# Attention and a two-layer feed-forward on one core: the last pair's first tile stored whole, and a new hand-written order of all operations

## The chip, the cores and the metric

The kernel runs on one core of one Trainium2 chip. The core has a matrix engine (TensorE, PE in the profile, with its weight loads shown apart as PEld), three engines for elementwise work (VectorE or DVE, ScalarE or ACT, GpSimd or POOL) and SyncE (SP), which only starts transfers. Each engine works through its own queue in order, and engines wait for each other by semaphores. Transfers (DMA) are started from the queues of SP, ACT and POOL. The metric is the device time of one execution in microseconds (us), lower is better.

## What is computed

Attention with a squared ReLU in place of a softmax, over 8 batches, 12 heads, 448 positions and head size 64; its output, as 3584 tokens of 768 features, goes through two weight matrices with a sigmoid-gated activation between them.

```
def _attn_ref(q, k, v):                       # each (8, 12, 448, 64)
    scores = scale * np.matmul(q, k.transpose(0, 1, 3, 2))
    attn = np.maximum(scores, 0.0) ** 2 / S
    return np.matmul(attn, v).astype(np.float32)

def _moe_ref(x, w_in, w_out):                 # (3584, 768), (768, 2048), (2048, 768)
    h = x @ w_in
    g = h * (1.0 / (1.0 + np.exp(-1.702 * h)))
    return (g @ w_out).astype(np.float32)
```

## The kernel before

**Units and batches.** Four heads of one batch make a unit u; there are 24 units, three to a batch. For each unit q and k are loaded, cast to fp16, transposed on TensorE (tq, tk) and copied out of PSUM (eq, ek). For each of seven row tiles j, TensorE makes the scores (s, four matmuls in 64x64 pieces of the array), ACT or DVE takes the ReLU of the two halves (r), ACT or DVE squares both at once (x), and after the seventh tile TensorE multiplies by v (a, 28 matmuls in 64x64 pieces). Two copies (e) bring the result into the batch's input for the feed-forward.

**First weight matrix.** For batch 0 it is a plain product: f (two matmuls of one third of the depth), then the activation g on ACT, then the widening v (scale and cast to fp16) on DVE or POOL into a ring buffer of two batches. For batches 1 to 7 it is a fast scheme with seven products in place of eight: sums of weight blocks (S, once) and of input blocks (T, per batch) on DVE, the products u (six matmuls each) on TensorE, a snapshot t of one bank on ACT or DVE, an addition b on DVE, then g and v.

**Second weight matrix.** The same scheme over pairs of 128-token tiles: sums W of weight blocks (once), sums A of the ring (per pair), the products p (eight matmuls each), snapshots h and final additions l into the output tile osb, and the stores o (a whole tile, on SP) or q (a part of a tile, on SP or ACT). A pair m covers the tiles m and m+1; the last pair is 26 with tiles 26 and 27. Its product p26.5 is split into two halves of 192 columns, p26.5.0 and p26.5.1, and l26.5 with it.

**The order.** `with tc.manual_schedule()` (from line 387 on) holds one long list of words, `words` (from line 430); `do` (line 404) issues them in exactly this order. Each engine's queue is the list's words for that engine, in the order of the list. A word is a name, its indices, an optional engine after a colon (`a` ACT, `d` DVE, `p` POOL) and, after an @, the PSUM banks that it takes into use. `r3.0.1` is the ReLU of unit 3, tile 0, half 1, on ACT (the default of r); `r3.0.0:d` is one on DVE; `s0.1@4.5` makes the scores of unit 0, tile 1 in banks 4 and 5. Without a suffix e, x, b, l, S, T, W and A are on DVE, r, t, h on ACT, g always on ACT, v on POOL. L loads q or k over SP, and K and Q cast what it loaded (default ACT for K, POOL for Q); j and V load with a cast over POOL's queue, jwa/jwb and jo the weights. A bank is taken again only after the operations that read it are through; buffers in SBUF (15 for at, 5 for gf, 3 for osb, 4 for v16 and so on) likewise.

The transposes come in two shapes: seven matmuls of 128x128 for units that were cast by K or Q, fourteen of 128x64 for units 1 to 5, which were loaded with a cast.

**The steps that the change touches at the end.** `store_part` (line 302) stores a part of a tile; its first index after the pair is h: 0 and 1 the halves of 384 columns, 2 and 3 quarters of 192. The index i picks the tile's upper or lower 64 rows, since these lie in different places of the output. With `:a` the store is started from ACT's queue, otherwise from SP's. `pair_snap` (line 362, word h) writes a scaled copy of a bank to osb, `pair_last` (line 366, word l) adds a bank to what osb holds; which of the two comes first on a piece of osb writes it, and the second one adds (`from_bank`, line 352). The end of the list, with the words of the last pair:

```
p26.4 l26.3 p26.6 h26.4:d h26.5 q27.1.1:a
q27.1.0 p26.5.0@4 q26.0.1:a l26.6 p26.5.1@3 q26.1.1:a q26.1.0 l26.5.0 q27.2.1:a
q27.2.0 l26.5.1 q27.3.1:a q27.3.0
```

Of the kernel before, what the change touches and what calls it, by code (L numbers as in the profile page):

```python
# [15 lines left out]
def kernel(  # L16
# [11 lines left out]
    NT, DM = out.shape  # L28
# [5 lines left out]
    NOUT = DM // 2  # L34
# [253 lines left out]
    lo, hi = slice(0, NOUT), slice(NOUT, DM)  # L288
# [13 lines left out]
    def store_part(e, p, m, h, i):  # L302
        b, j = divmod(2 * m + i, J)
        r0 = b * S + j
        c = slice(h * NOUT, (h + 1) * NOUT) if h < 2 else slice(
            (h - 2) * NOUT // 2, (h - 1) * NOUT // 2)
        (nc.scalar if e == "a" else nc.sync).dma_start(
            out=out[r0:r0 + 63 * J + 1:J, c], in_=osb[m][64 * i:64 * i + 64, c])
# [78 lines left out]
    with tc.manual_schedule():  # L387
# [34 lines left out]
        def zeros(e, p, n):  # L422
# [8 lines left out]
            "Lq0 Lk0 z9@0 jq1 jk1 I V0 V1 z1 Q0:d z1 z1 z1 z1 z1 z1 tq0@1 K0:d eq0:a tk0@2 ek0 "  # L431
            "tq1@3 jk2 eq1 s0.1@4.5 jq2 s0.4@6.7 s0.5@0.1 r0.1.1 r0.1.0:d s0.0@2.3 jq3 r0.5.1 "
            "r0.5.0:d s0.6@5.4 r0.0.0 r0.0.1:d r0.6.0 s0.2@1.0 x0.5 r0.2.0 s0.3@2.3 tk1@5 r0.2.1 "
            "x0.1 r0.4.0 ek1 jk3 r0.3.0 x0.2 r0.6.1 s1.6@1.0 jwb0 s1.3@6.5 r0.3.1:d r1.6.0 jwa0 "
            "r1.6.1 x0.6 s1.2@2.4 s1.0@3.1 r1.3.0 x0.3 r1.2.0 s1.5@0.6 x0.0 r0.4.1 r1.5.0:d r1.2.1 "
            "s1.1@2.7 r1.0.1 r1.0.0:d tk2@0 r1.1.0 x0.4 s1.4@4.1 r1.3.1 tq2@3 ek2 r1.1.1 a0@2.5 jq4 "
            "eq2 x1.3:a x1.2 jk4 r1.5.1 r1.4.0:d tq3@0 e0.0:a V2 x1.0 s2.3@7.3 e0.1:a tk3@6 jwb2 "
            "eq3 r2.3.1 s2.2@4.2 r1.4.1 ek3 s2.1@5.0 jwa2 r2.3.0 x1.1 s3.3@3.1 r2.1.1 jwa1 s2.4@6.7 "
            "x1.6 r2.2.0 jwb1 x1.4 r3.3.1 x1.5 a1@0.4 r2.1.0 jk5 r2.4.1 r3.3.0:d r2.2.1 jq5 "
            "s2.0@1.5 r2.4.0:d s3.2@7.3 e1.1:a f0.1.0@2 V3 e1.0 r2.0.0 s2.5@6.4 r2.0.1 r3.2.1:d "  # L440
            "jwb3 s3.4@0.1 r3.2.0 f0.1.1 r2.5.1:d r2.5.0 f0.0.0@5 jwa3 x2.2 f0.0.1 r3.4.0 V4 x2.0 "
            "s2.6@3.7 r3.4.1 s3.0@4.6 r2.6.0 x2.1 tk4@0 V5 r3.0.1 f0.2.0@1 r3.0.0:d r2.6.1 jo0.0 "
# [12 lines left out]
            "x5.3 V6 f0.12.0@1 r5.6.1 K6:d f0.14.0@5 v0.4 r5.2.1 f0.12.1 r5.6.0:d Lk7 x5.0:a "
            "u1.1.0@3 x5.1 u1.0.0@2 r5.2.0 x5.6 r5.4.0 f0.13.0@0 x5.5 u1.2.0@7 e4.1:a S3.1 x5.2:a "
            "f0.12.2 x5.4 f0.14.1 g0.12 a5@4.6 S3.3 Q6:d S1.2 Lq8 tq6@1 e5.0:a v0.12:d f0.13.1 T1.1 "
            "e5.1:a f0.14.2 t1.1.0:d tk6@4 g0.14 T1.2 f0.13.2 S0.3 u1.0.1@6 g0.13 S3.2 p0.0@5 "
            "t1.0.0 v0.13 eq6:a b1.0.1 v0.14 S1.4 u1.0.2 ek6:a S3.4 u1.1.1@0 g1.0.1 T1.3 u1.3.0@1 "
            "t1.0.2 b1.1.1 v1.0.1 u1.1.2 S1.3 g1.1.1 u1.0.4 W0.1 t1.1.2 u1.0.3 W2.1 t1.0.4 u1.1.4 "  # L460
            "K7 b1.0.3 u1.1.3 W1.1 g1.0.3 Lk8 f0.9.0@4 T1.4 t1.1.4 u1.0.6 v1.0.3 Q8:a b1.1.3 f0.9.1 "
            "v1.1.1 f0.9.2 b1.0.6 Lq7 u1.1.6 W3.1 g0.9 u1.3.1@6 g1.1.3 b1.1.6 v0.9 t1.2.0 u1.1.5 "
            "v1.1.3:d t1.3.0 A0.1@0 u1.2.1@4 g1.0.6 W2.3 u1.2.2 g1.1.6 v1.0.6 b1.2.1 tk7@0 t1.2.2 "
            "u1.0.5 b1.3.1 v1.1.6 W1.3 u1.3.2 g1.3.1 W0.3 g1.2.1 u1.2.4 v1.3.1 W3.2 t1.3.2 u1.3.3 "
            "t1.2.4 u1.2.3 A0.2@1 ek7:a u1.2.5 W3.3 g1.0.5 b1.2.3 u1.3.4 K8 v1.0.5 h0.0:d tq8@0 "
            "W2.2 u1.2.6 g1.2.5 Lk9 W1.2 eq8:a p0.1@2 v1.2.5 b1.2.6 W0.2 t1.3.4 v1.2.1 W2.4 "
            "s6.0@7.0 p0.2 r6.0.0 Q7 l0.1 g1.1.5 b1.3.3 r6.0.1 V8 s6.4@4.7 Lq9 W0.4 h0.2 s6.2@3.0 "
            "p0.3 A0.3 r6.2.0 r6.4.1 W3.4 r6.2.1 W1.4 r6.4.0 s6.5@3.7 v1.1.5:d tq7@0 r6.5.0 A0.4 "
            "p0.4 r6.5.1 eq7 x6.2:a x6.5 s6.6@4.3 x6.0 h0.4 s6.3@7.0 Q9 r6.6.1 u1.3.5 r6.3.1:d "
            "r6.3.0 tk8@3 l0.3 g1.3.5 p0.5 K9:p Lq10 r6.6.0:d x6.4:a ek8 v1.3.5 Lk11 x6.3:a "  # L470
            "s7.4@0.7 l0.5 s6.1@1.4 u1.3.6 r7.4.0 r6.1.1:d o1 r7.4.1 x6.6 s7.0@3.5 s7.1@0.4 r6.1.0 "
            "p0.6 b1.3.6 r7.0.1 x6.1 r7.1.0 r7.0.0 x7.4 s7.3@7.1 r7.1.1 s7.2@6.5 l0.6 a6@0.3 r7.2.0 "
            "x7.1 o0 r7.3.0 A2.1@0 r7.2.1 s7.6@4.2 x7.0 r7.3.1 s8.4@6.7 V10 tq9@5 r7.6.0 r7.6.1:d "
            "tk9@1 Q10 e6.1:a r8.4.0:d p2.0@4 eq9:a ek9 K11:p r8.4.1:d x7.2:a s8.2@2.3 x7.6 "
            "s7.5@6.5 Lk10 p2.1@1 r7.5.1 r7.5.0:d Lq11 e6.0:a x7.3 x7.5:a r8.2.0:d s8.1@7.5 a7@6.0 "
            "r8.2.1:d r8.1.1 r8.1.0 A2.2@1 h2.0 x8.1 s8.6@2.3 s8.3@5.7 e7.0:a p2.2 r8.3.0:d e7.1:a "
            "K10:p r8.6.0 r8.6.1:d r8.3.1 l2.1 V13 s9.0@6.5 Lk12 x8.6:a s8.0@0.2 x8.3 s8.5@3.7 p2.3 "
            "r8.0.0:d r8.0.1 r9.0.1 x8.2 r8.5.1 x8.0 tk11@0 r8.5.0 u2.1.0@2 x8.4 ek11:a x8.5 a8@5.7 "
# [152 lines left out]
```

## Time and profile before

| | us |
|---|---|
| median of 3 runs | 375.39 (374.13 to 375.76) |
| the profiled execution, its own time | 374.8 |
| its span, first to last instruction | 373.0 |
| mean granted TensorE clock, share of full | 0.998 |
| start of the first and of the last matmul group on TensorE (zp; second half of p26.5) | 1.12 and 367.55 |
| last elementwise instruction (l26.5.1 on DVE), start and length | 368.41, 0.36 |

A busy share is taken over the whole span, while the stages have different limits: attention and the first layer's plain product at the start, the fast scheme with attention beside it in the middle, and only the second matrix at the end. The mean length of one matmul in the page (326 ns for an ox matmul, say) is longer than the spacing of two of them, since matmuls are pipelined; how long a group keeps TensorE is therefore read from start to start. In the 40 slices of the page, DMA and the three engines PE, DVE and ACT stand at 9 tenths in most of the first fifth of the span, and ACT and DVE have less and less to do towards the end:

```
PE   8899999999999999999999999999999999999995
DVE  3999999999999998898899699978998889767762
ACT  3999989999988999789978997899994897636310
DMA  9999999357673437360572524620520301110344
```

### The profile page before, as it was taken

The numbers are of one execution on the slowest core, as the hardware profiler recorded it, in microseconds if no ns is written. First come the engines' busy times: TensorE is split into PE (matmuls) and PEld (weight loads), VectorE is DVE, ScalarE is ACT, GpSimd is POOL, SyncE is SP. The second block draws the span as 40 slices with busy tenths as digits, with TensorE's granted clock in tenths as the row PEclk, the third lists the DMA queues.
The fourth block names the chain that finished last, engine by engine and source line by source line (L and its number), as shares of the span: only waits on it lengthen the run. The fifth ranks groups of instructions, "written<-read, shape, count | busy, mean of one in ns | idle before, by whom it ended". The sixth has DMA issues, their size and how long they took to land.

```text
span 373.0 us, 9514 instructions
## 1 busy us (share of the span) xinstructions
PE 365.6 (98%) x3830; PEld 252.9 (68%) x3830; DVE 321.5 (86%) x602; ACT 297.3 (80%) x568; POOL 114.3 (31%) x164
## 2 busy tenths in 40 slices
PE   8899999999999999999999999999999999999995
PEld 4444568855589555886568965599568855788663
DVE  3999999999999998898899699978998889767762
ACT  3999989999988999789978997899994897636310
POOL 6464523452334424231341322335400410012000
PEclk9999999999999999999999999999999999999999
DMA  9999999357673437360572524620520301110344
GB/s 195 171 188 206 238 232 232 135 138 203 166 196 99 120 62 209 112 160 2 134 199 34 177 28 114 183 37 2 95 43 2 86 2 41 45 44 16 71 99 114
DMA packets 31981, 43.16 MB, mean 116 GB/s; under 512 B 2368, under 2 KB 28608, under 8 KB 31936
## 3 DMA queue, kind: packets, MB, share of 16 engines
q1 hardware_dynamic: 14928, 28.06, 25.7%
q0 software_dynamic: 16608, 14.09, 25.2%
q8 instruction: 30, 0.49, 0.5%
q10 hardware_dynamic: 400, 0.39, 0.4%
q14 instruction: 15, 0.12, 0.1%
HBM read 45.61 MB, written 11.01 MB: 152 GB/s over the span
## 4 chain that ended last, share of the span: by engine, by line
PE 95%; DVE 3%; ACT 1%; issue 0%
PE ox L188 35%; PE hx L188 30%; PE sc L141 10%; PE av L172 8%; PE ht L208 5%; PE tr L117 4%; PE zp L426 1%; DVE at L85 1%; DVE at L152 1%; PE tr L122 1%; ACT at L154 1%; DVE kT L80 0%; DVE qT L80 0%; DVE osb L357 0%; DVE wT L417 0%
## 5 line engine op out<-in xcount | busy, mean ns | idle before, releaser
L154 ACT ACTIVATE at<-sc 128x448 f16<-128x448 f32 x229 | 112.2, 567 | 10.6 <-PE sc L141 9.9
L198 POOL TENSOR_SCALAR ring<-gf 128x448 f16<-128x448 f32 x87 | 53.7, 617 | 151.0 <-ACT gf L195 144.0
L188 PE MATMUL ox<-wout,ring 128*128 128x384 f16 x448 | 80.3, 326 | 0.0
L188 PEld LDWEIGHTS <-ring 128*128 128x128 f16 x568 | 53.0, 98 | 37.5 <-issue 7.6
L152 DVE TENSOR_SCALAR at<-sc 128x448 f16<-128x448 f32 x107 | 63.9, 617 | 5.8 <-PE sc L141 5.6
L85 DVE TENSOR_TENSOR at<-at 128x896 f16<-128x896 f16 x107 | 65.5, 636 | 1.7 <-ACT at L154 1.6
L188 PEld LDWEIGHTS <-win 128*128 128x128 f16 x672 | 63.8, 98 | 4.4 <-issue 2.1
L85 DVE TENSOR_TENSOR gf<-hx,gf 128x448 f32<-128x448 f32 x84 | 50.8, 620 | 9.9 <-PE hx L188 5.2
L160 ACT ACTIVATE at<-at 128x896 f16<-128x896 f16 x61 | 57.7, 960 | 0.5
L188 PE MATMUL hx<-xb,win 128*128 128x224 f16 x504 | 57.0, 259 | 0.0
L195 ACT ACTIVATE gf<-gf 128x448 f32<-128x448 f32 x84 | 47.2, 578 | 11.5 <-DVE gf L85 11.3
L141 PE MATMUL sc<-qT,kT 64*64 64x448 f16 x672 | 50.2, 359 | 1.6 <-DVE kT L80 1.1
L188 PEld LDWEIGHTS <-winS 128*128 128x128 f16 x504 | 48.0, 98 | 3.1 <-issue 1.3
L76 ACT ACTIVATE gf<-hx 128x448 f32<-128x448 f32 x60 | 31.8, 541 | 13.4 <-PE hx L188 11.4
L188 PE MATMUL ox<-wT,asum 128*128 128x384 f16 x224 | 40.6, 327 | 0.0
L188 PE MATMUL hx<-T,winS 128*128 128x224 f16 x336 | 39.7, 259 | 0.0
L172 PE MATMUL av<-at,v 64*64 64x448 f16 x672 | 36.2, 350 | 0.1
L141 PEld LDWEIGHTS <-kT 64*64 64x64 f16 x672 | 17.1, 105 | 23.9 <-issue 17.3
L188 PEld LDWEIGHTS <-asum 128*128 128x128 f16 x224 | 20.8, 98 | 16.6 <-issue 3.4
L357 DVE SCALAR_TENSOR_TENSOR osb<-ox,osb 128x384 f32<-128x384 f32 (+1 forms) x44 | 23.8, 541 | 5.9 <-PE ox L188 5.7
L78 ACT ACTIVATE osb<-ox 128x384 f32<-128x384 f32 x26 | 13.1, 503 | 19.6 <-PE ox L188 16.8
L172 PEld LDWEIGHTS <-v 64*64 64x64 f16 x672 | 20.4, 107 | 11.6 <-issue 1.5
(61 smaller groups left out, 426.0 us busy)
## 6 DMA issues: line engine op xcount, KB each, us to landing
out_dram<-osb SPq DMA_DIRECT2D x52, 192.0 KB, 3.0
qst<-in_q_dram SPq DMA_DIRECT2D x19, 448.0 KB, 4.5
kst<-in_k_dram SPq DMA_DIRECT2D x19, 448.0 KB, 4.2
v<-in_v_dram POOLq DMA_DIRECT2D x24, 224.0 KB, 5.0
win<-in_moe_w_in_dram POOLq DMA_DIRECT2D x8, 384.0 KB, 9.7
wout<-in_moe_w_out_dram POOLq DMA_DIRECT2D x4, 768.0 KB, 20.6
q<-in_q_dram POOLq DMA_DIRECT2D x5, 224.0 KB, 5.9
k<-in_k_dram POOLq DMA_DIRECT2D x5, 224.0 KB, 5.4
```

The costliest lines, as they stand in the source:

```text
L76: nc.scalar.activation(out=o, in_=i, func=AF.Copy)
L85: eng[e].tensor_tensor(out=o, in0=x, in1=y, op=op)
L141: nc.tensor.matmul(out=sc[a][c, 0:S], lhsT=st["kT"][r, j, c], rhs=st["qT"][r, :, c], start=True, stop=True)
L152: nc.vector.tensor_scalar(out=o, in0=i, scalar1=0.0, scalar2=None, op0=ALU.max)
L154: nc.scalar.activation(out=o, in_=i, func=AF.Relu)
L160: nc.scalar.activation(out=at, in_=at, func=AF.Square)
L172: nc.tensor.matmul(out=av[s][64 * a:64 * a + 64, 0:S], lhsT=v16[r, a, 64 * j:64 * j + 64], rhs=at[r, a, :], start=(j == 0), stop=(j == J - 1))
L188: nc.tensor.matmul(out=o, lhsT=lhs(i), rhs=rhs(i), start=start and i == 0, stop=i == n - 1, skip_group_check=True)
L195: nc.scalar.activation(out=o, in_=i, func=AF.Gelu_apprx_sigmoid, scale=1.0 / SC)
L198: eng[e].tensor_scalar(out=o, in0=i, scalar1=SC, scalar2=1.0, op0=ALU.mult, op1=ALU.mult)
L208: nc.tensor.matmul(out=hp[g, f][:, 0:S], lhsT=w[:, i, fo:fo + 128], rhs=xts[g][:, i, :], start=i == 0, stop=i == NK - 1)
L357: nc.vector.scalar_tensor_tensor(out=o, in0=x, scalar=1.0 / SC, in1=o, op0=ALU.mult, op1=ALU.add)
```

## The change

Two things are changed. `store_part` can store all 768 columns of a tile (index 4), and the four stores of tile 26's halves (two on SP, two on ACT) become two stores of the whole width (one on SP, one on ACT). And the list of words is a new one throughout: the same operations otherwise (1989 words in place of 1991, 591 of them on TensorE in both), in another sequence, in other banks, and some on another engine:

| word | before | after |
|---|---|---|
| ek (copy of transposed k) | 9 ACT, 15 DVE | 4 ACT, 20 DVE |
| eq (copy of transposed q) | 10 ACT, 14 DVE | 11 ACT, 13 DVE |
| x (square) | 61 ACT, 107 DVE | 57 ACT, 111 DVE |
| r (ReLU) | 229 ACT, 107 DVE | 231 ACT, 105 DVE |
| h (snapshot for osb) | 26 ACT, 17 DVE | 30 ACT, 13 DVE |
| v (widening) | 87 POOL, 41 DVE | 94 POOL, 34 DVE |
| K and Q (casts) | 7 ACT, 6 DVE, 25 POOL | 5 ACT, 9 DVE, 24 POOL |

The diff, cut to the function, the beginning and the end of the list:

```diff
     def store_part(e, p, m, h, i):
         b, j = divmod(2 * m + i, J)
         r0 = b * S + j
-        c = slice(h * NOUT, (h + 1) * NOUT) if h < 2 else slice(
+        c = {0: lo, 1: hi, 4: slice(0, DM)}.get(h) or slice(
             (h - 2) * NOUT // 2, (h - 1) * NOUT // 2)
         (nc.scalar if e == "a" else nc.sync).dma_start(
             out=out[r0:r0 + 63 * J + 1:J, c], in_=osb[m][64 * i:64 * i + 64, c])
...
-            "Lq0 Lk0 z9@0 jq1 jk1 I V0 V1 z1 Q0:d z1 z1 z1 z1 z1 z1 tq0@1 K0:d eq0:a tk0@2 ek0 "
-            "tq1@3 jk2 eq1 s0.1@4.5 jq2 s0.4@6.7 s0.5@0.1 r0.1.1 r0.1.0:d s0.0@2.3 jq3 r0.5.1 "
-            "r0.5.0:d s0.6@5.4 r0.0.0 r0.0.1:d r0.6.0 s0.2@1.0 x0.5 r0.2.0 s0.3@2.3 tk1@5 r0.2.1 "
-            "x0.1 r0.4.0 ek1 jk3 r0.3.0 x0.2 r0.6.1 s1.6@1.0 jwb0 s1.3@6.5 r0.3.1:d r1.6.0 jwa0 "
...
-            "A26.1@0 p24.5 p26.0@6 l24.5 l24.3 A26.2@1 o25 p26.1@2 h26.0:d p24.6 l26.1 q26.0.0 "
-            "p26.2 l24.6 A26.4 o24 A26.3 p26.3 h26.2 p26.4 l26.3 p26.6 h26.4:d h26.5 q27.1.1:a "
-            "q27.1.0 p26.5.0@4 q26.0.1:a l26.6 p26.5.1@3 q26.1.1:a q26.1.0 l26.5.0 q27.2.1:a "
-            "q27.2.0 l26.5.1 q27.3.1:a q27.3.0"
...
+            "z9@0 z1 z1 z1 Lq0 Q0:d z1 z1 Lk0 K0:d z1 z1 jq1 I tq0@1 eq0:a tk0@2 ek0 tq1@3 eq1 "
+            "s0.1@4.5 r0.1.1 s0.6@6.7 jk1 r0.1.0:d s0.0@0.1 r0.0.0 V0 V1 s0.5@2.3 r0.0.1:d s0.3@5.4 "
+            "r0.6.0 jk2 jq2 r0.5.0:d r0.3.0 s0.2@0.1 x0.1 r0.3.1:d r0.2.1 jq3 r0.2.0 r0.5.1 tk1@6 "
+            "ek1 r0.6.1 s0.4@2.5 x0.0 x0.6 r0.4.0 s1.2@4.1 r0.4.1 x0.2 s1.1@0.3 r1.2.1 x0.4 jk3 "
...
+            "v7.3.3:d h24.2 p24.4 g7.1.6 p24.3 h24.4 p24.5 o23 A24.4 b7.3.6 g7.3.6 v7.3.6 l24.3 "
+            "p24.6 v7.1.6 A26.1@0 A26.3 l24.6 o24 l24.5 o25 A26.2@1 p26.0@6 p26.1@4 h26.0 l26.1 "
+            "p26.2 p26.3 A26.4 h26.2 p26.4 l26.3 h26.4:d q27.1.1:a q27.1.0 p26.6 l26.6 q26.4.1:a "
+            "q26.4.0 p26.5.0@5 h26.5 l26.5.0 q27.2.1:a q27.2.0 p26.5.1@0 l26.5.1 q27.3.0 q27.3.1:a"
```

## The prediction

> **What bounds the kernel now.** I read the busy line of the page first, then busy time by three stretches, then the chain of waits for the cost of single groups, and last the timeline of both ends.
>
> ```profile
> PE 365.6 (98%) x3830; PEld 252.9 (68%) x3830; DVE 321.5 (86%) x602; ACT 297.3 (80%) x568; POOL 114.3 (31%) x164
> ...
> 0.00:24.00 24.00, 21.19 (x264) 11.20 (x264) 18.22 (x35) 18.08 (x39) 15.01 (x26) 1.00 1.08 183
> 24.00:349.00 325.00, 324.99 (x3443) 229.70 (x3441) 289.95 (x543) 276.13 (x525) 99.29 (x138) 1.00 0.49 112
> 349.00:373.00 24.00, 19.38 (x128) 12.01 (x125) 13.37 (x26) 3.07 (x6) 0.00 (x0) 0.97 0.40 100
> ```
>
> The columns after the stretch are PE, PEld, DVE, ACT and POOL busy, then clock, DMA share, GB/s. From 24 to 349 us TensorE is busy for 324.99 of 325 us. So there only the work on TensorE itself counts; what another engine saves there is worth nothing unless TensorE was waiting for it. The three terms of the sum are therefore TensorE's own list, the head (0 to 24) and the tail (after the last matmul).
>
> **Term 1, TensorE's list.** Every word of the hand-written order issues a fixed number of matmuls (s 4, a 28, f 2, u 6, p 8, tk/tq 7 or 14), and these add up to the 3830 of the page for both orders: nothing is added or removed on TensorE, only its sequence changes. Start to start, one word takes 1.300 us (p), 0.575 (u), 0.378 (f), 1.324 (a), 0.19 to 0.21 (s), 0.39 (seven transposes) and 0.42 (fourteen), when its neighbours use the same shape of the array. Three shapes occur: 128x128 (p, u, f, seven transposes), 64x64 (s, a), 128x64 (fourteen transposes). At a change of shape there is a surcharge, and the chain of waits shows it (start us, us, what):
>
> ```profile
> 178.38 2.60 PE ox L188 x16
> 180.98 0.69 PE sc L141 x12
> 181.67 2.71 PE ox L188 x16
> 184.37 0.50 PE sc L141 x8
> 184.88 1.32 PE av L172 x28
> 186.20 0.38 PE sc L141 x8
> 186.58 1.41 PE ox L188 x8
> ```
>
> Sixteen ox matmuls take 2.60 us entered from a 128x128 group and 2.71 entered from sc; eight sc take 0.38 after av (same shape) and 0.50 after ox. So a change costs some 0.11 us. Counted in the two orders, there are 136 changes before and 130 after (128x128 to 64x64 and back 118 against 116, those with 128x64 18 against 14): 6 x 0.11 = 0.66 us less. Adding up word by word with the usual spacing for each pair of neighbours gives the same: the last product would start at 362.64 in the old order and at 361.98 in the new. **Term 1: -0.66** (bounds -0.66 and 0, if the spacings did not carry over).
>
> **Term 2, the head.** In the trace the last product starts at 367.55, which is 4.91 later than 362.64. All of that arises before 24 us; after that no spacing is more than 0.04 us over its usual value. The timeline of the head shows who is full (start, busy, engine, what, count, idle before it):
>
> ```profile
> 8.32 8.40 ACT L154 ACTIVATE at<-sc 128x448 f16<-128x448 f32 x19 [0.61 <-PE sc L141]
> ...
> 11.64 3.33 PE L141 MATMUL sc<-qT,kT 64*64 64x448 f16 x24 [0.72 <-DVE kT L80]
> ...
> 18.73 4.07 ACT L154 ACTIVATE at<-sc 128x448 f16<-128x448 f32 x9
> 19.77 2.22 DVE L85 TENSOR_TENSOR at<-at 128x896 f16<-128x896 f16 x4
> 20.66 1.96 PE L172 MATMUL av<-at,v 64*64 64x448 f16 x28
> ```
>
> ACT and DVE run back to back, while 24 sc matmuls that need 6 x 0.2 = 1.2 us take 3.33. What stands ahead of a matmul on those two engines, in order, thus gives the earliest time. Spacings from the trace: on ACT relu 0.424, square 0.84, evacuation 0.425, transpose evacuation 0.80; on DVE all of these 0.535. Old order: ahead of s3.4's bank DVE does 30 operations (7 transpose evacuations, 9 relu, 13 squares, e1.0), 30 x 0.535 = 16.0; from its first at 7.18, plus 0.15 for the hand-over, that is 23.36, against 18.74 on TensorE's own list: 4.62 late, 4.91 measured, so 0.29 is small waits. New order: ahead of s3.4 DVE does 35 (7, 11 relu, 16 squares, e1.0), 18.7: 26.04 against 21.21, 4.83 late. ACT ahead of a1 does 25 relu, one square, two evacuations and eq0, 13.09, from an effective 7.52: 20.76 against 15.99, 4.77 late. The head does not shrink. With the same small waits or none it ends 4.83 to 5.12 late, against 4.91: I take 5.0. **Term 2: +0.1** (-0.08 to +0.21).
>
> The loads of the head keep their sequence on POOL's queue, apart from jk1 behind the identity (0.5 us) and swaps inside jwa0/jwb0, jwa1/jwb1 and jq5/jk5. Nearest cover: the first w_in block landed at 20.3 and f0.0.0 needs it at 17.82 + 4.8 = 22.6; tk1 now comes after six scores, and its data landed at 7.8. SP's first loads are unchanged.
>
> **Moved engines, at no price.** ACT sheds 5 transpose evacuations, 4 squares, 2 casts and gains 4 snapshots, 2 relu, 1 transpose evacuation: about -5.8 us; DVE gains about 1.2 (5 transpose evacuations, 4 squares and 3 casts more; 7 widens, 4 snapshots, 2 relu and 1 transpose evacuation fewer); POOL gets 7 more widens (7 x 0.62) and a cast less. TensorE hides all of this in 24 to 349, where DVE has 35 us and ACT 49 us spare; if that cover were gone, the DVE part would cost 1.2. On POOL v0.0 and v0.1 now stand ahead of V6, which feeds a6 only at about 85 us; on SP the loads and stores swap places by one or two.
>
> **Term 3, the tail.** Two stores fewer: tile 26 went out in four halves of 96 KB and now goes in two wholes of 192 KB. But the order on ACT changes too: h26.5, the snapshot that both l26.5 halves add to, stood ahead of all ACT stores, and now stands behind q27.1.1 and q26.4.1.
>
> ```profile
> 366.38 3.12 SPq L307 DMA_DIRECT2D out_dram<-osb  x4
> 366.39 0.49 ACT L78 ACTIVATE osb<-ox 128x384 f32<-128x384 f32 x1 [2.70 <-DVE osb L357]
> 366.39 3.63 ACTq L307 DMA_DIRECT2D out_dram<-osb  x5
> 366.89 1.48 PE L188 MATMUL ox<-wT,ring 128*128 128x192 f16 x16
> 367.16 1.02 DVE L357 SCALAR_TENSOR_TENSOR osb<-ox,osb 128x384 f32<-128x384 f32 x2 [0.81 <-PE ox L188]
> 368.41 0.36 DVE L357 SCALAR_TENSOR_TENSOR osb<-ox,osb 128x192 f32<-128x192 f32 x1 [0.23 <-PE ox L188]
> ```
>
> ACT's five stores hold its queue for 0.47 to 0.79 us each, one after the other; the last one starts at 369.56, 0.79 after its data (368.41 + 0.36). Count from the start of the last product (367.55): l26.6 ends at +0.17; q26.4.1 waits for it and starts at +0.26 (the old q26.1.1 did), holding ACT to +0.73...+1.05; behind it wait h26.5, 0.49, to +1.22...1.54, and then DVE with the two l26.5 halves (0.36 each, 0.28 apart) to +1.9...2.2. Meanwhile q27.2.1 starts on ACT at +1.66...1.98, holds it for 0.47 to 0.64, and q27.3.1 follows at +2.17...2.66, against +2.00 before; the old trace has a further pause of 0.34 ahead of its last store, which makes +3.0 the worst. From there to the end I keep the old landing (2.3 us) and closing (1.1). If a store that waits did not hold ACT, the last would go out when the old data were ready, +1.25. Bounds -0.75 to +1.0; I take the middle of what the rows give, **term 3: +0.45**.
>
> The Trainium skill ("DMA: Bandwidth & Descriptors", "Issuing engines are not separate DMA queues" and the anatomy's table of the fixed cost) calls the sequencer's time to start a DMA usually small, and gives about 50 ns for dispatch. The five ACT stores of this trace, 0.47 to 0.79 us, say otherwise; by the page h26.5 would hardly be held up and the whole sum would be about -1.3 instead of -0.1.
>
> **Sum.** -0.66 + 0.1 + 0.45 = -0.11. The profiled execution took 374.8 us with a span of 373.0 and 1.8 around it; it would become 374.7. It lies 0.6 under the median of the runs, 375.39, so the median would be 375.3. Bounds together: -1.5 to +1.2.
>
> **Rivals.** *The tail is free.* A waiting store does not hold ACT, and all bounds fall low: -0.66 - 0.08 - 0.75 = -1.5, 373.9. For it: the store instructions overlap the ACTIVATE at 366.39. Against it: the stores themselves start one after the other. *A longer tail and no saving:* 0 + 0.21 + 1.0 = +1.2, 376.6; against it, the surcharge repeats at every change of shape in the trace. *Slower: ACT late in batch 1.* The new order's tightest ACT operation of this stage is t1.0.2, whose bank u1.0.4 overwrites: 103 operations, 48.9 us, from 7.52 end at 56.5 (56.6 with the hand-over), against 54.6 + 4.9 = 59.5 on TensorE. ACT may lose 2.9 us in waits by then; in the old trace its waits from 8.3 to 66 us sum to 2.4. From 2.9 on, each microsecond is one of TensorE's; if the new sequence doubled the waits to 4.9, +2.0: 377.3. Against it: the old order had only 2.0 to lose at its tightest place (r5.2.0 before u1.2.0), and TensorE was not late there.
>
> **Numbers.** Forecast 0.52, free tail 0.20, longer tail 0.14, ACT late 0.14. About what this kernel's measurement can tell from no change is 0.5%, 1.9 us: 373.5 to 377.3. Faster than that: 0.11, the part of the free tail that the spread of the runs (374.13 to 375.76) carries past the line; slower: the late ACT, 0.14; within: 0.75. The range, 373.6 to 376.9, holds the bounds of the sum and the spread, and leaves out the late ACT and the edge of the free tail. The forecast's own is 374.4 to 376.2.
>
> **What would show it.** Term 1: last product about 0.5 earlier, no spacing in 24 to 349 above its usual value. Term 2: DVE and ACT still without idle time from 8.3 to 24. Term 3: h26.5 behind a store on ACT, the last l26.5 about 0.7 to 1.0 later against the last product than before. A wait of TensorE for ACT or DVE between 24 and 349, or an ACT that runs h26.5 during q26.4.1's wait, would prove me wrong.

## The result, and the profile after

The changed kernel takes 378.75 us (median of 4 runs, 377.97 to 382.11) beside 375.43 for the kernel before (4 runs, 374.13 to 375.76) on the same chip; the ratio is 1.0122, 95% interval 1.0095 to 1.0149. The forecast was 375.3 with a range to 376.9: the change is slower, and the time lies outside the range.

The profiled execution of the changed kernel took 377.97 us with a span of 376.2 (before: 374.8 and 373.0), at a granted clock of 0.997 (before 0.998). Its difference of 3.2 us is taken apart the way the prediction put the time together: word by word on TensorE, each spacing against its usual value for that pair of neighbours. A second profiled execution of the same kernel, taken later, stands beside it (span 377.8).

| us | before | after | after, once more |
|---|---|---|---|
| TensorE's own list: last product would start at | 362.64 | 361.98 | 361.98 |
| late by 6.2 us, against before | 0 | -0.39 | +0.02 |
| late from 6.2 to 24 | 4.99 | 5.20 | 5.51 |
| late from 24 to 34 | -0.07 | 0.08 | 0.19 |
| **late from 34 to 48** | **-0.08** | **2.65** | **2.97** |
| late from 48 to the last product | 0.06 | 0.89 | 1.40 |
| last product starts | 367.55 | 370.42 | 372.06 |
| from there to the end of the span | 5.46 | 5.76 | 5.76 |

So one stretch of 14 us holds most of it. Busy time by stretch shows it at once. The columns are as in the prediction: PE, PEld, DVE, ACT, POOL busy, then clock, DMA share and GB/s. First the changed kernel:

```profile
0.00:24.00 24.00, 20.70 (x270) 11.10 (x270) 18.57 (x36) 18.47 (x40) 14.48 (x26) 1.00 1.08 185
24.00:349.00 325.00, 323.53 (x3413) 227.24 (x3410) 292.81 (x540) 266.67 (x514) 104.92 (x142) 1.00 0.49 112
...
34.00:48.00 14.00, 12.96 (x121) 6.47 (x120) 11.43 (x23) 10.54 (x23) 9.46 (x11) 1.00 1.24 231
```

and the kernel before for the last of these:

```profile
34.00:48.00 14.00, 14.00 (x173) 7.17 (x174) 13.17 (x26) 13.79 (x29) 7.66 (x10) 1.00 1.24 231
```

From 34 to 48 us TensorE falls from 14.00 to 12.96 busy, and ACT (13.79 to 10.54) and DVE (13.17 to 11.43) fall too, although they have work; only POOL rises. Three engines go idle together while a fourth is busier: that points at something on the fourth, and the chain of waits below bears it out. The timeline of the changed kernel (start, busy, engine, line, operation, count, in brackets the idle time before it and what ended it) shows what:

```profile
32.85 1.83 POOL L379 DMA_DIRECT2D wout<-in_moe_w_out_dram  x2 [1.18 <-DMA win<-in_moe_w_in_dram]
...
34.93 0.87 POOL L379 DMA_DIRECT2D wout<-in_moe_w_out_dram  x1 [0.24 <-DMA k<-in_k_dram]
...
36.22 0.87 POOL L379 DMA_DIRECT2D wout<-in_moe_w_out_dram  x1 [0.42 <-DMA v<-in_v_dram]
37.17 1.20 POOL L198 TENSOR_SCALAR ring<-gf 128x448 f16<-128x448 f32 x2
37.76 0.54 ACT L195 ACTIVATE gf<-ht 128x448 f32<-128x448 f32 x1 [2.66 <-POOL ring L198]
38.35 0.58 PE L122 MATMUL tr<-ident,k 128*64 128x128 f16 x14 [0.43 <-ACT gf L195]
39.21 0.62 DVE L85 TENSOR_TENSOR at<-at 128x896 f16<-128x896 f16 x1 [2.57 <-ACT at L154]
40.88 1.95 PE L172 MATMUL av<-at,v 64*64 64x448 f16 x28 [0.40 <-ACT gf L195]
```

The four loads of the second weight matrix (the words jo) are started from POOL's queue, and by the profile their starts wait until earlier loads (a block of w_in, k, v) have landed. Behind them on the same queue stand the widens v0.0 and v0.1, which the change took from DVE to POOL. They run at 37.17. Until then none of the five gf buffers comes free (g0.0 to g0.3 and g0.8 hold them), so ACT stands for 2.66 us ahead of its next activation, g0.10, the squares and ReLUs behind it are late, DVE stands for 2.57 us for one of them, and TensorE for a3. In the kernel before, three of the first four widens ran on DVE, the first at 32.09, while POOL was still busy with the same loads:

```profile
32.09 0.39 DVE L198 TENSOR_SCALAR ring<-gf 128x448 f16<-128x448 f32 x1
...
36.72 0.88 POOL L379 DMA_DIRECT2D wout<-in_moe_w_out_dram  x1 [0.22 <-issue]
38.79 0.70 POOL L100 DMA_DIRECT2D v<-in_v_dram  x1 [1.20 <-PE tr L122]
39.56 1.46 POOL L198 TENSOR_SCALAR ring<-gf 128x448 f16<-128x448 f32 x2
```

The chain of waits of the changed kernel (start, length, what) runs through the same place; the piece of it shown with the prediction was nothing but TensorE:

```profile
23.88 12.05 DMA v<-in_v_dram
35.93 0.28 issue
36.22 0.87 POOL wout L379
...
37.17 0.57 POOL ring L198
...
37.76 0.03 ACT gf L195
...
38.62 0.56 ACT at L154
...
41.32 1.51 PE av L172 x26
```

It starts with a V load issued at 23.88 that lands at 35.93. The start of a weight load waits for that landing, a widen for the start, ACT for the widen. In the second execution that last start came at 37.36, 1.14 later; 0.83 of this the whole program was late by there, so the start came 0.31 later against TensorE's own place. ACT stood 2.98 us, 0.32 more, and TensorE lost 2.97, 0.32 more: the loss moves with that start.

The tail of the changed kernel, by the timeline (its last product starts at 370.42):

```profile
369.25 4.00 SPq L307 DMA_DIRECT2D out_dram<-osb  x4
369.25 1.87 ACTq L307 DMA_DIRECT2D out_dram<-osb  x2
...
371.23 0.49 ACT L78 ACTIVATE osb<-ox 128x384 f32<-128x384 f32 x1 [4.67 <-DVE osb L357]
371.75 0.62 DVE L357 SCALAR_TENSOR_TENSOR osb<-ox,osb 128x192 f32<-128x192 f32 x2 [1.16 <-ACT osb L78]
372.14 1.38 ACTq L307 DMA_DIRECT2D out_dram<-osb  x2
```

The snapshot h26.5, an ACTIVATE of 0.49 us, stands behind two stores on ACT, and DVE waits 1.16 us for it, as the prediction had it.

### The profile page after: what moved, and what is told of

The parts are those of the page before. It is cut to its first block, busy times and chain, and to the rows that moved or that the text cites. A ratio compares the mean times of both kernels' runs of the same rounds, so it can differ in the third digit from the quotient of the medians.

```text
span 376.2 us, 9523 instructions
## 1 busy us (share of the span) xinstructions
PE 366.5 (97%) x3830; PEld 252.8 (67%) x3830; DVE 325.0 (86%) x600; ACT 291.1 (77%) x564; POOL 121.1 (32%) x170
## 4 chain that ended last, share of the span: by engine, by line
PE 87%; DMA 6%; DVE 2%; issue 2%; POOL 1%; ACT 1%; ACTq 0%; DVEq 0%; POOLq 0%
PE ox L188 34%; PE hx L188 29%; PE sc L141 8%; PE av L172 8%; PE tr L117 4%; DMA v<-in_v_dram 3%; PE ht L208 2%; DMA k<-in_k_dram 2%; DMA q<-in_q_dram 1%; PE zp L426 1%; DVE T L85 1%; POOL ring L198 0%; DVE osb L357 0%; ACT at L154 0%; DVE osb L82 0%
## 5 line engine op out<-in xcount | busy, mean ns | idle before, releaser
L154 ACT ACTIVATE at<-sc 128x448 f16<-128x448 f32 x231 | 113.5, 580 | 12.9 <-PE sc L141 12.7
L198 POOL TENSOR_SCALAR ring<-gf 128x448 f16<-128x448 f32 x94 | 59.5, 633 | 174.9 <-ACT gf L195 163.6
L85 DVE TENSOR_TENSOR at<-at 128x896 f16<-128x896 f16 x111 | 68.1, 639 | 4.8 <-ACT at L154 4.3
L152 DVE TENSOR_SCALAR at<-sc 128x448 f16<-128x448 f32 x105 | 62.1, 616 | 5.3 <-PE sc L141 5.1
L188 PE MATMUL hx<-xb,win 128*128 128x224 f16 x504 | 57.8, 259 | 0.4 <-DVE kT L80 0.4
L160 ACT ACTIVATE at<-at 128x896 f16<-128x896 f16 x57 | 54.6, 970 | 0.6 <-DVE at L152 0.4
L78 ACT ACTIVATE osb<-ox 128x384 f32<-128x384 f32 x30 | 14.9, 496 | 19.3 <-PE ox L188 14.3
```

Source lines behind the costliest of these rows:

```text
L85: eng[e].tensor_tensor(out=o, in0=x, in1=y, op=op)
L152: nc.vector.tensor_scalar(out=o, in0=i, scalar1=0.0, scalar2=None, op0=ALU.max)
L154: nc.scalar.activation(out=o, in_=i, func=AF.Relu)
L160: nc.scalar.activation(out=at, in_=at, func=AF.Square)
L188: nc.tensor.matmul(out=o, lhsT=lhs(i), rhs=rhs(i), start=start and i == 0, stop=i == n - 1, skip_group_check=True)
L198: eng[e].tensor_scalar(out=o, in0=i, scalar1=SC, scalar2=1.0, op0=ALU.mult, op1=ALU.mult)
```

## The experiments

All ratios are to the kernel before on the same chip. Each edit is one to the list of words, if nothing else is said.

### Where the first widens stand

The first theory: v0.0 and v0.1 behind the weight loads on POOL cost the 2.65 us. Rivals: the late landings themselves hold TensorE, wherever the widens stand; or DVE is too full in the new order of that stretch.

**Widens back on DVE.**

```diff
- s4.3@3.5 v0.0 r4.3.0:d s3.1@7.2 r4.3.1 v0.1 V6
+ s4.3@3.5 v0.0:d r4.3.0:d s3.1@7.2 r4.3.1 v0.1:d V6
```

> The changed kernel with two widens, v0.0 and v0.1, given back to DVE; nothing else differs. Theory A (POOL's queue): on POOL they stand behind the four wout issues, the last of which starts only at 36.22 us; until they run, the five gf buffers are full and ACT stands 2.66 us ahead of g0.10, and TensorE loses 2.65 us between 37 and 43. Then ACT's wait of 2.66 us goes, TensorE's loss in 37 to 43 falls to under 0.5, and the span falls from 376.2 to about 373.6. Rival B (late data: the chain of waits names the load of v that lands at 35.9): the loads are the same, so the loss stays at 2.65 and the span at 376.2. Rival C (DVE is too full in the new order): DVE gets 0.6 us more just there, so the loss grows to about 3.2 and the span to 376.8.

376.51 us, ratio 1.0043 (1.0026 to 1.0060), span 374.7. TensorE is late by 0.37 us from 34 to 48, where it was 2.65, and 0.30 of this comes at the very end, at 47.8. The time does not come down to that of before: besides 47.8, this execution is late by 0.3 to 0.5 us at each of three other places (33.2, 151.8, 195.4), and the tail is that of the changed kernel.

**Two of the four weight loads behind the widens.**

```diff
- ek4 jo1.1 f0.2.2 f0.3.2 jo0.1 x3.3
+ ek4 f0.2.2 f0.3.2 x3.3
...
- r4.3.1 v0.1 V6
+ r4.3.1 v0.1 jo1.1 jo0.1 V6
```

> The changed kernel with the last two wout issues (jo1.1 and jo0.1) moved behind v0.0 and v0.1 in the list; the widens stay on POOL. Theory A: v0.0 can run at about 34.7 us instead of 37.17, ACT's wait shrinks from 2.66 to under 0.6, the loss in 37 to 43 falls to 0.3 to 1.0 (v0.3 and V6 now stand behind the two issues), span 373.8 to 374.6. Rival B: loss 2.65, span 376.2. Rival C: POOL and DVE do the same work as before, so loss 2.65, span 376.2.

377.81 us, ratio 1.0065 (1.0039 to 1.0091), the profiled execution 376.27 with a span of 374.4; late from 34 to 48: 0.79. The two widens, still on POOL, now run at 34.49 instead of 37.17:

```profile
34.49 1.56 POOL L198 TENSOR_SCALAR ring<-gf 128x448 f16<-128x448 f32 x2
```

So POOL is not too slow for them; what stands ahead of them is. The 0.79 is that of the fastest of four executions: the other three took 377.70 to 378.00, so they may have been later here.

**The kernel before with its two widens on POOL.**

```diff
- s4.1@3.6 v0.1:d f0.10.0@2 ... r3.1.0 v0.0:d f0.8.0@1
+ s4.1@3.6 v0.1 f0.10.0@2 ... r3.1.0 v0.0 f0.8.0@1
```

> The kernel before with v0.0 and v0.1 moved from DVE to POOL, the reverse of the first run. Theory A: in the old list they stand on POOL behind V14, which starts at 38.79 us, and v0.3; v0.0 would end at about 41, ACT would stand some 5 us ahead of g0.8 or g0.10, and TensorE would lose 3 to 6 us between 34 and 46; span 376 to 379. Rivals B and C: no loss there, span 373.0 or a little less, since DVE is relieved of 0.6 us.

376.9 us, ratio 1.0047 (1.0025 to 1.0070), span 375.1. The move alone makes the old order slower, but by less than I expected: late by 1.48 us from 34 to 48, not 3 to 6. (Another 1.37 us come behind 48, 0.54 and 0.34 of them at 83.6 and 85.3; what makes those is not shown.) The timeline of this kernel:

```profile
36.03 0.87 POOL L379 DMA_DIRECT2D wout<-in_moe_w_out_dram  x1 [0.27 <-DMA v<-in_v_dram]
38.21 0.70 POOL L100 DMA_DIRECT2D v<-in_v_dram  x1 [1.31 <-PE tr L122]
38.98 3.00 POOL L198 TENSOR_SCALAR ring<-gf 128x448 f16<-128x448 f32 x4
39.58 0.54 ACT L195 ACTIVATE gf<-ht 128x448 f32<-128x448 f32 x1 [1.53 <-POOL ring L198]
40.17 1.51 PE L172 MATMUL av<-at,v 64*64 64x448 f16 x26 [1.16 <-ACT gf L195]
```

The same mechanism, with a V load ahead of the widens as well: they run only at 38.98. But ACT reaches the activation that needs a free buffer later, and so stands 1.53 us instead of 2.66. The price of a late widen is not its delay; it is the delay less what ACT has left to do before it needs the buffer.

**All four weight loads behind three widens.**

```diff
- f0.2.1 jo0.0 r3.0.1 ... r2.5.0 jo1.0 r3.6.1 ... ek4 jo1.1 f0.2.2 f0.3.2 jo0.1 x3.3
+ f0.2.1 r3.0.1 ... r2.5.0 r3.6.1 ... ek4 f0.2.2 f0.3.2 x3.3
- r4.3.1 v0.1 V6 ... f0.6.1 v0.3 f0.6.2
+ r4.3.1 v0.1 v0.3 jo0.0 jo1.0 jo1.1 jo0.1 V6 ... f0.6.1 f0.6.2
```

> The changed kernel with v0.0, v0.1 and v0.3 ahead of all four wout issues on POOL; every operation stays on its engine. Theory A, sharpened: what hurts is any widen behind an issue on POOL that waits for a landing. Then no gf buffer depends on a landing: TensorE's loss in 34 to 48 us is under 0.4 (2.65 in the changed kernel, 0.79 with two of the issues moved), the last product starts at about 368.0, the span is 373.7 to 374.2, and the runs without a saved trace agree with the profiled one. Rival (the sequence of TensorE or DVE's load is what loses there): the loss stays over 1.

375.88 us, ratio 1.0035 (1.0019 to 1.0050), span 373.8. From 34 to 48 TensorE is busy throughout (late by -0.05):

```profile
31.56 2.08 POOL L198 TENSOR_SCALAR ring<-gf 128x448 f16<-128x448 f32 x3 [0.29 <-ACT gf L195]
33.70 3.56 POOL L379 DMA_DIRECT2D wout<-in_moe_w_out_dram  x4
...
34.00:48.00 14.00, 14.00 (x170) 7.35 (x166) 13.50 (x26) 13.26 (x28) 7.40 (x10) 1.00 1.24 231
```

The widens keep their engine and run at 31.56; the first weight load starts at 33.70 instead of 32.85, and the weights are in time. That settles the 2.65 us: not the widens' engine and not late weights, but the order on POOL's queue. What is left of 1.0035 is the tail (5.76) and late places of 0.25, 0.50 and 0.23 us at 83.5, 105.9 and 161.0.

### The tail

**The snapshot ahead of ACT's stores.**

```diff
- h26.4:d q27.1.1:a q27.1.0 ... p26.5.0@5 h26.5 l26.5.0
+ h26.4:d h26.5 q27.1.1:a q27.1.0 ... p26.5.0@5 l26.5.0
```

> The changed kernel with h26.5 moved back ahead of both ACT stores of its neighbourhood. Theory T (a store that waits holds ACT): h26.5 runs before the last product starts, the last l26.5 ends about 1.2 us after the start of the last product instead of 1.95, the last store starts at 1.3 to 1.7 after it instead of 2.6, span 375.0 to 375.4. Rival: the last store is set by the chain of stores on ACT or by landing, whatever h26.5 does, span 376.2.

378.72 us, ratio 1.0097 (1.0069 to 1.0126), span 375.7. A miss: the span should have been 375.0 to 375.4. The snapshot is early:

```profile
368.88 0.49 ACT L78 ACTIVATE osb<-ox 128x384 f32<-128x384 f32 x1 [2.70 <-DVE osb L357]
368.89 3.80 ACTq L307 DMA_DIRECT2D out_dram<-osb  x4
370.91 0.36 DVE L357 SCALAR_TENSOR_TENSOR osb<-ox,osb 128x192 f32<-128x192 f32 x1 [0.23 <-PE ox L188]
```

and the last store starts 1.75 us after the start of the last product (changed kernel 2.31, before 2.00), but it lands at 4.37 (4.48 and 4.31). Counted from the same point, the end comes at 5.64 instead of 5.76: 0.12 for the snapshot. By their landings, the two stores of 192 KB that start at 0.20 take until 2.9 and 3.6; in the kernel before, the stores of 96 KB that start there are through at 2.36 and 2.67. The late quarter stores land behind them.

**The stores of before in the new order.** The kernel with all weight loads behind three widens, and tile 26 in four halves again with the snapshot first (below: the kernel of halves):

```diff
- q27.1.0 p26.6 l26.6 q26.4.1:a q26.4.0
+ q27.1.0 q26.0.1:a p26.6 l26.6 q26.1.1:a q26.1.0
```

(with q26.0.0 behind l26.1 and h26.5 behind h26.4)

> The previous kernel with tile 26 stored in four halves again, and h26.5 ahead of the ACT stores, as in the kernel before. Theory W (with h26.5 first, what sets the end is how late the bytes are: the whole stores put 384 KB behind the last product's start, the halves 192 KB): last landing at +4.2 to +4.4 from the start of the last product and the end at +5.4 to +5.5, against 5.76 in the changed kernel and 5.64 with h26.5 first and whole stores; span 0.25 to 0.35 below the previous kernel's. Rival (the stores are hidden; only h26.5's place counts): +5.64.

374.59 us, ratio 0.9999 (0.9989 to 1.0010), span 372.7; from the last product's start to the end 4.81 us, where the same kernel with whole stores has 5.76. That is more than I expected (5.4 to 5.5).

```profile
366.73 3.43 ACTq L307 DMA_DIRECT2D out_dram<-osb  x5
```

The last of these starts 1.70 after the start of the last product and lands at 3.66.

**The stores of the change in the old order.** The kernel before with the whole store alone:

```diff
- q27.1.0 p26.5.0@4 q26.0.1:a l26.6 p26.5.1@3 q26.1.1:a q26.1.0
+ q27.1.0 p26.5.0@4 l26.6 p26.5.1@3 q26.4.1:a q26.4.0
```

(and without q26.0.0; `store_part` as changed)

> The kernel before with tile 26 stored whole and nothing else: the first of the two parts of the change alone. Theory W: two stores fewer shorten ACT's row of stores by 0.6 us (last one issued at 1.4 to 1.8 after the start of the last product instead of 2.0), but their bytes come later, so the end stays at +5.4 to +5.7 (5.46 before); no difference that can be measured, span 372.9 to 373.3. Rival (the row of stores on ACT sets the end): +4.9 to +5.2, span 372.5 to 372.8.

375.08 us, ratio 1.0016 (1.0002 to 1.0030). The end comes 5.69 us after the start of the last product, its last store starting at 1.75 and landing at 4.42. So the first-named part of the change, two stores fewer, makes the end later: by 0.9 us against the halves in the new order, by 0.2 against the profiled execution before, which is a bad one of its kind: the same stores in the kernel of halves end at 4.81, with the last store landing 1.95 after its start instead of 2.31, and without the pause of 0.34 us ahead of it. In the execution before, fifteen of the sixteen parts of the last store had landed by 3.86 and one came at 4.31. A packet of 8 KB of instructions stood beside it from 2.70 to 3.35. The old kernel with its widens on POOL ends at 5.16 and has such a packet too, from 2.25 to 2.73; the five executions with halves in the new order end at 4.79 to 4.81 and have none there. It may have held the store; that is not shown.

### The small places that remain

**Three copies and squares on ACT.** In the kernel of halves late places of 0.23 to 0.37 us were left at s7.1 to p0.6 (83.2), u3.0.2 (150.9), u3.0.5 (160.5) and p10.4 (194.5). Is DVE just too full there, since the change gave it more transpose copies?

```diff
- ek8 ... ek10 ... x12.6
+ ek8:a ... ek10:a ... x12.6:a
```

> The kernel with halves (second of this call) with three operations moved from DVE to ACT: ek8, ek10 and x12.6. Theory D (the small losses after 84 us are DVE's, which is too full at these places in the new order): the losses at s7.1 (0.25), u2.2.1 (0.52 in the changed kernel's trace) and u3.0.5 (0.23) go, 0.5 to 1.0 in all; span 372.4 to 373.2, that is level with the kernel before or up to 0.5 below it. Rival (they move to the next tight place): the sum of the losses after 48 us stays within 0.3 of the previous kernel's.

375.66 us, ratio 1.0027 (1.0011 to 1.0042): worse than without the move (0.9999). At p0.6 TensorE is now late by 0.64, and new places come at 110.9 and 114.4; u3.0.2 keeps its 0.31; u3.0.5 and p10.4 are in time. Behind 48 us TensorE is late by 1.8 in all, where it was 1.1. So neither theory came true: the losses did not go, and they did not stay the same.

The traces show what p0.6 waits for. The new order puts the transposes tk8 into bank 4 (3 before), which s7.1 takes next, so s7.1 has to wait for ek8, the copy out of that bank. In the changed kernel:

```profile
85.48 0.61 DVE L80 COPY kT<-tr 128x896 f16<-128x896 f16 x1
...
86.15 0.11 PEld L141 LDWEIGHTS <-kT 64*64 64x64 f16 x2 [0.30 <-issue]
```

The copy ends at 86.09, and the last three matmuls of s7.1 start at 86.15. In all eleven executions of the new order they start 0.05 to 0.06 us after ek8 ends, also in this one, where ek8 runs on ACT and takes longer.

**Sums clear of POOL's casts.** The timeline of the kernel of halves shows what happens at u3.0.2: a sum on DVE (T3.2) that takes 0.50 us elsewhere takes 1.26 beside a cast on POOL. A sum of the ring ahead of p10.4 does the same (1.41, elsewhere 0.68).

```profile
149.90 0.92 POOL L80 CAST q<-qst 128x896 f16<-128x896 f32 x1 [8.64 <-DMA qst<-in_q_dram]
149.92 1.26 DVE L85 TENSOR_TENSOR T<-xb,T 128x672 f16<-128x672 f16 x1
...
192.51 1.20 POOL L80 CAST q<-qst 128x896 f16<-128x896 f32 x1
192.84 1.41 DVE L85 TENSOR_TENSOR ring<-ring 128x1024 f16<-128x1024 f16 x1
```

```diff
- e11.0:a T3.3 u3.0.0@2 T3.2 t3.0.0:d ... h6.4:d t3.2.0
+ e11.0:a u3.0.0@2 T3.2 t3.0.0:d ... h6.4:d T3.3 t3.2.0
- l6.5 Q18 b3.0.6 u3.3.1@0 g3.2.3 v3.2.3 t3.1.4
+ l6.5 b3.0.6 u3.3.1@0 g3.2.3 v3.2.3 Q18 t3.1.4
- g3.3.6 Q19 h10.0 ... x14.0 v3.3.6 r15.3.0
+ g3.3.6 h10.0 ... x14.0 v3.3.6 Q19 r15.3.0
```

> The kernel with the widens ahead of the wout loads and the last store in halves, with five words moved so that a sum of two fp16 tiles on VectorE no longer runs beside a cast on POOL: the sum T3.3 behind T3.2, Q18 behind the next widen, Q19 behind the next widen. Nothing else is changed, and no work. Theory: a VectorE sum whose two operands lie in SBUF stands still while POOL computes, so T3.2 (1.26 us before), T3.4 (1.23) and the ring sum at 192.8 (1.41) fall back to 0.50, 0.50 and 0.68 us, the three late places behind them (u3.0.2 0.34, u3.0.5 0.23, p10.4 0.37 us) go, and the profiled execution is 0.7 to 0.95 us shorter than the same kernel without the move (span 371.8 to 372.0; ratio to the kernel before 0.997 to 0.9985). Rival: the sums are long for another reason (their operands, the order on VectorE), so they stay at 1.2 to 1.4 us where they now run and TensorE is late by the same 0.9 us: ratio as that of the kernel without the move, within 0.1 per cent. Second rival: the sums get short but the late casts hold up the loads behind them, and TensorE waits for q or k instead: span 372.5 or more with a late transposition (tq17, tk18 or tq19).

374.95 us, ratio 1.0003 (0.9985 to 1.0022), span 372.9. Both the theory and its second rival come true. The sums are short, also at their new places on DVE:

```profile
149.40 0.51 DVE L85 TENSOR_TENSOR T<-xb,T 128x672 f16<-128x672 f16 x1
149.74 0.96 POOL L80 CAST q<-qst 128x896 f16<-128x896 f32 x1 [8.58 <-DMA qst<-in_q_dram]
...
159.62 0.50 DVE L85 TENSOR_TENSOR T<-xb,T 128x672 f16<-128x672 f16 x1
...
163.22 0.93 POOL L80 CAST q<-qst 128x896 f16<-128x896 f32 x1
...
172.68 1.52 PE L172 MATMUL av<-at,v 64*64 64x448 f16 x28 [0.97 <-DMA v<-in_v_dram]
```

and the three late places are gone. But Q18 at 163.22 frees its staging tile later, the two loads that wait for it start at 164.17 instead of 162.67, and the V load issued among them comes too late for a12: TensorE stands, 1.16 us over the usual spacing. What was won was given back by a transfer, though not by the transposition that I had named.

**The kernel of halves once more**, for the comparison on the same chip:

> The kernel without the moved sums once more, on the same chip, for the comparison: ratio 0.999 to 1.001, the three late places u3.0.2, u3.0.5 and p10.4 there again at 0.2 to 0.4 us each if they come from the program's order; if they were chance of one execution, they are elsewhere.

374.94 us, ratio 1.0001 (0.9993 to 1.0010). The late places at p0.6 and u3.0.5 came again with 0.24 and 0.23; p10.4 with 0.12 instead of 0.37, and u3.0.2 not at all. So two are of the order, and two come and go. For u3.0.2 the trace shows why: the cast starts when a q load has landed, and here it started 0.13 us behind the sum T3.2, not 0.02 ahead of it. The sum took 0.50 us and the cast 1.16, instead of 1.26 and 0.92.

**Q18 back, the other moves kept.**

```diff
- v3.2.3 Q18 t3.1.4
+ v3.2.3 t3.1.4
- l6.5 b3.0.6
+ l6.5 Q18 b3.0.6
```

> The kernel with the moved sums and casts, but Q18 back where it stood, so that its staging tile comes free at 160.9 us and the loads Lq17 and Lk18 start 1.5 us sooner again. Theory (a cast that is later holds the two loads, these crowd the load V12, and a12 is late by 1.16 us): the late place at a12 goes, T3.4 is long again (1.2 us) with 0.23 us behind it at u3.0.5, the sums T3.2 and the ring sum stay short; the last product starts at 367.0 to 367.5, the span is 371.7 to 372.3, ratio to the kernel before 0.997 to 0.999. Rival: a12's wait is chance of one execution, then the span is that of the kernel with Q18 moved, 372.7 to 373.1, and the ratio is 1.000 to 1.001.

374.15 us, ratio 0.9991 (0.9980 to 1.0002), span 372.2. a12 is in time again, T3.4 long again with 0.23 us behind it, the last product starts at 367.38. The sum ahead of p10.4 did not stay short (1.04 us, 0.68 expected), but p10.4 is in time. This is the fastest version by median, 0.43 us below the kernel before, but its interval reaches 1: it can't be told from it. A kernel clearly faster than the one before did not come out.

**The changed kernel once more.**

> The changed kernel once more. Ratio 1.010 to 1.015. If what stands ahead of v0.0 on POOL is the cause, TensorE is late by 2.3 to 3.0 us between 34 and 48 us again and the last product starts near 370.4; the late places at 108.2 (0.52 us) and 163.4 (0.23 us) come again if they are of the program's order, and the loss between 24 and 48 moves by more than 0.5 us only if the landing of the V load at 35.9 us moves.

379.53 us, ratio 1.0127 (1.0109 to 1.0146), span 377.8. Late by 2.97 from 34 to 48; the last product starts at 372.06, later than I expected: 0.83 of the 1.64 arose up to 34 us, 0.32 with the V load that lands later, and 0.51 behind 48 us, where two places (49.7 and 51.9) add 0.65. The place at 163.4 came again (165.1, 0.23), the one at 108.2 did not.

## Why the prediction was wrong

**Term 1, TensorE's list, was right.** The usual spacings, added up over the new order, put the last product at 361.98, and from 200 us on, in both of its executions, no spacing is more than 0.1 over its usual value. Behind 48 us the spacings outside the late places add up to within 0.12 us of the forecast in both. With most of the waits taken out, in the run with Q18 back, the last product starts earlier than before (367.38 against 367.55), though it is still 5.40 late against 4.91.

**Term 2, the head, held as far as can be told.** Up to 24 us, the start among it, the changed kernel is late by 4.81 in one execution and 5.53 in the other, against 4.99: -0.18 and +0.54 around the forecast +0.1. The kernel of halves, whose beginning is the same, gave 4.74 and 5.39 in its two executions, so this is scatter of one order and not a price of it. Over all traces the start of the new order is late by 4.66 to 5.53 (eleven), that of the old one by 4.55 to 4.99 (three): a difference of 0.1 can't be read from that.

**"Moved engines, at no price" is the step that failed.** It said that TensorE hides these moves from 24 to 349 us, since DVE has 35 us and ACT 49 us spare there, and for POOL it looked only at what stands behind v0.0 and v0.1 (V6 and a6, at 85 us). Two things were left out. What stands *ahead* of them: four starts of loads that wait for landings. And who waits for *them*: ACT, for a gf buffer, of which there are five. That gave 2.65 us in the first execution and 2.97 in the second, and moving the loads behind the widens took it to -0.05. The spare time was a mean over 325 us; from 34 to 48 the old trace had ACT busy for 13.79 of 14 us, so there it had 0.2 us to spare, not 49. The sentence on what it costs if the cover is gone priced DVE's work (1.2), not a wait.

The same step missed the smaller losses. The profiled execution of the changed kernel is late by a further 0.89 us behind 48 us, the second by 1.40. In the first 0.75, in the second 0.53 of this are sums on DVE that stand beside a cast or widen on POOL (last section), at places where TensorE waits for them:

- u3.0.5 (0.23) is late in the nine executions of the new order in which T3.4 took 1.22 to 1.23 us, and in time in the two in which it took 0.50. The run that moved Q18 away and the one that put it back show that the cast makes it.
- u3.0.2 (0.30 in the second execution) is late by 0.30 to 0.34 in the five executions in which T3.2 took 1.23 to 1.27, and in time in the six in which it took 0.50 to 0.51. Only two of these six are the runs that moved the sum; in the other four it started level with the cast Q16 or up to 0.13 us ahead of it, in the five 0.02 to 0.07 behind it.
- u2.2.1, the 0.52 at 108.2, came in two executions, the first of the changed kernel and the one with all loads behind three widens. These are the two in which T2.1 took 1.05 us or more beside K12 and T2.4 0.86 or more beside a widen, instead of 0.50 to 0.77 and 0.50; u2.2.1 starts 0.06 after the copy ek10, which stands behind these sums.

The 0.25 us at p0.6 are of another kind, a bank: s7.1 waits for ek8. The 0.65 us of the second execution at 49.7 and 51.9 stay open.

**Term 3, the tail: right sign, wrong mechanism, and the size by luck.** +0.45 was forecast and +0.30 measured (5.76 against 5.46). That ACT's queue holds h26.5 was right: it starts 0.80 us after the start of the last product, by the forecast 0.73 to 1.05, and the last store of ACT at 2.31 (2.17 to 2.66). In the changed kernel the landing then took 2.17, near the 2.3 that was kept, so the sum comes out. But the snapshot is worth only 0.12: when it is early, the last store starts 0.56 earlier and takes 2.62 to land. "From there to the end I keep the old landing (2.3 us)" is the sentence that failed: here the landing of a late store depends on the bytes ahead of it. With halves it took 1.95. The 0.30 is small only because the execution before was a bad one; against the kernel of halves the changed tail costs 0.95. The prediction counted two stores fewer as two starts fewer, and never as two transfers that are twice as long at the worst moment. The 50 ns that the prediction cites from the Trainium skill ("DMA: Bandwidth & Descriptors") stand under "Anatomy of one DMA — SWDGE (gpsimd) path", and "usually small" under "Issuing engines are not separate DMA queues" is meant relative to the transfer. These stores were started by ACT and SP.

**The rivals.** "ACT late in batch 1" had the right kind (an ACT that loses more in waits than TensorE has to give) and even nearly the right size (+2.0, where TensorE lost 2.65). But it looked for the place at 56 us, by adding up ACT's operations. The wait came from 35.1 to 37.8, from another queue, and ACT's total up to there would not have shown it. It had 0.14; the chance was too small because ACT's waits of the old order (2.4 us) were carried over to an order in which another engine frees its buffers.

**What the sum is without the two faults.** With the loads behind the widens, the stores in halves, and a sum and a cast moved, the profiled execution takes 373.97 against 374.8 before. But 0.65 us of this lie behind the last product, where the execution before was a bad one; the last product starts 0.17 earlier. By the medians the two kernels can't be told apart (0.9991, 0.9980 to 1.0002). So a gain of the new order is not shown, though its list on TensorE is shorter by 0.66.

## What to carry to other kernels

When an operation moves to another engine, read that engine's queue ahead of it, line by line, and look for anything that waits for a landing; then name who waits for the operation's buffer, and ask how long that one can go on without it in that very stretch. Busy shares over a long stretch say nothing about a stretch of 5 us. Near the end, count the bytes still in flight when the last small store starts, and not only the number of starts: in this kernel four halves ended 0.8 to 0.9 us sooner than two whole stores.

## What the runs showed of the hardware

**A sum on VectorE and an instruction on POOL can shut each other out, and the one that starts first wins.** TENSOR_TENSOR with two fp16 operands in SBUF takes 0.50 us (128x672), 0.62 (128x896) or 0.68 (128x1024) alone, and up to 1.26, 1.33 and 1.41 beside a cast or widen on POOL. Operations that read PSUM keep their length beside one (0.62 us for a ReLU from PSUM and for the addition of a bank, with POOL busy or idle). In the run with the moved sums, T3.2 and T3.4 fell from 1.26 and 1.23 to 0.51 and 0.50 with the same operands on the same engine. The length fits waiting to the end of POOL's instruction and then running in full: a cast from 149.90 to 150.82, then 0.50, would end the sum at 151.32; it ended at 151.18. It also goes the other way: in the changed kernel T3.2 started at 153.15, 0.08 ahead of the cast, and took 0.50, while the cast took 1.21 instead of 0.92.

The Trainium skill says as much ("SBUF — State Buffer", "Who interferes with whom"): a VectorE instruction with two SBUF inputs and a GpSimd instruction that reads SBUF need the same port, and the one that issues first has it for its whole length. These traces agree, with the lengths above.

**A start of a load on POOL's queue that waits holds POOL's arithmetic.** At 36.22 a weight load waits for a V load to land, and two widens with all their data ready stand behind it. The Trainium skill has this too ("DMA: Bandwidth & Descriptors", "Anatomy of one DMA — SWDGE (gpsimd) path"): the wait is made by the engine that issues, ahead of dispatch. Here its price was 2.65 us. Why the start of a weight load waits for a V load, whose data it does not use, no run here shows.

**The start of a small store has no fixed price.** Quarter stores of 48 KB hold their queue for 0.47 to 0.92 us behind the start of the last product (the kernel with the snapshot first: 0.55, 0.86, 0.89 and 0.92; the changed one: 0.47, 0.50, 0.56 and 0.78). The longest ones overlap a start on the other queue, but two that start together at 1.71 take 0.47 and 0.50, so what sets it stays open.
